# Memory attention with stationary queries, a list scheduler for background work, and no unread matmuls

## The chip, the cores and the metric

One core of one Trainium2 chip. The metric is device time in microseconds (us) of one execution. "Clock" is the share of the TensorE clock that was granted during the execution, as the trace records it.

ScalarE does the exponentials, TensorE (PE) the matmuls, VectorE (DVE) the rest of the arithmetic, GpSimd (POOL) the masks. PE writes to eight PSUM banks of 128 x 512 f32.

## The reference, cut to what matters

Four layers over 2048 tokens of width 512, 32 heads of 16: A, B, A, B. Each is `x + layer(layernorm(x))`. B is full attention. A is attention within four segments of 512 tokens, causal, mixed by a gate with a read-out of a memory that the earlier segments filled.

```python
# A, for each segment s
p = softmax(q_s @ k_s.T * scale + causal_mask);  a_dot = p @ v_s
a_mem = (phi(q_s) @ M) / (phi(q_s) @ z + 1e-6)          # phi(t) = t + 1 if t > 0 else exp(t)
o = g * a_mem + (1 - g) * a_dot
M += phi(k_s).T @ v_s;  z += phi(k_s).sum(over tokens)
# B
o = softmax(q @ k.T * scale) @ v
```

## The kernel before

A Python program places every instruction of every engine beforehand. It keeps a model clock for each engine (`sc.t["pe"]` and so on), a price for each operation, and derives the semaphore waits from buffers and banks. Scores are made transposed, 128 keys by 512 queries a tile. Two or three tiles (of different heads, on different rows of the array) form a group; one exponential on ScalarE empties the group into SBUF. Two sets of banks alternate, so scores can be one group ahead of the exponential. The softmax sum comes from a 17th column of ones in the values. There are 4736 tiles.

```python
def emit_group(self, tiles, mode):      # scores of 2 or 3 tiles, then their exponential
    ...
    sc.add("pe", ... e.matmul(out, lhsT, rhs, start=True, stop=True) ..., cost=(SC0 if first else SC1))
    o = sc.add("act", lambda e: e.activation(dst, src, ACT.Exp, scale=float(SCALE)), ..., cost=0.065 + W / 1200.0)

while pos < len(stream):                # the main loop
    ...                                 # tiles in a fixed order; what they need is forced if it isn't there
    self.emit_group(tiles, m)
    dl = sc.t["act"] - SC0 - 0.1        # the last moment for the next scores, by the model
    self.fill(dl)                       # values (PV), projections and the rest, until then
    while warm and (2 * util + u1) / 3 < UTIL and sc.t["pe"] + MMC < dl:
        if not self.dummy():            # a 512-column matmul that nobody reads, to keep PE's clock up
            break
```

In `fill`, a projection is a thread that places one matmul at a time and holds its bank meanwhile. A group of value matmuls is placed as soon as the model has its exponentials done. Both go in front of the next scores as long as the model still has those in time.

The softmax here doesn't subtract the row's maximum and nothing guards it: scores larger than these inputs give would overflow.

## Time and profile before

| | |
|---|---|
| time | 2681.61 us, median of 2 runs (2669.08 to 2694.13) |
| ScalarE busy | 2256 us of 2696 (84%) |
| exponentials | 1644, of which 1448 with 1536 columns |
| exponentials waiting for scores | 330 us |
| mean clock | 0.75 |

From the page of the old kernel: busy time of each engine; then, in 40 slices of the span, ScalarE's share and the clock, in tenths; then the chain of waits that ended last.

```profile
PE 2296.5 (85%) x12630; PEld 567.9 (21%) x12630; DVE 715.0 (27%) x1572; ACT 2256.1 (84%) x1731; POOL 237.2 (9%) x568
ACT  2666776998999777777898878679999999999998
PEclk9668866999999875668898778579955565555555
PE 46%; ACT 33%; DVE 11%; issue 5%; DMA 3%; POOL 1%; SPq 1%; ACTq 0%; POOLq 0%; DVEq 0%
ACT pT L966 32%; PE ps L959 13%; PE ps L1047 12%; PE ps L1066 12%; PE ps L609 9%; DMA xT<-xn 2%; DVE lnst L641 1%; DVE T L1098 1%; DVE x_tok L863 1%; SPq L350 1%; DVE oT L1155 1%; PE ps L1085 1%; POOL pT L989 1%; DVE T L1088 1%; DVE q L624 1%
```

L959 are score matmuls, L966 exponentials, L1047 value matmuls, L609 projections, L1066 unread matmuls. ScalarE is the engine with the most to do besides PE, and the chain passes through PE more than through ScalarE: something on PE keeps the exponentials waiting.

Groups of ScalarE instructions of the old kernel, by shape (count, busy us, mean ns of one, idle us before them and its cause):

```profile
L966 ACT ACTIVATE pT<-ps 128x1536 bf16<-128x1536 f32 x1448 | 2030.4, 1451 | 289.6 <-PE ps L959 274.8 <-ACT pT L966 2.2 <-issue 1.4
L966 ACT ACTIVATE pT<-ps 128x1024 bf16<-128x1024 f32 x196 | 201.7, 1029 | 59.0 <-PE ps L959 54.7 <-POOL pT L989 2.5 <-issue 0.3
```

Busy time in stretches of 100 us of the old kernel. The columns are PE, weight loads, DVE, ScalarE and POOL with their instruction counts, then the clock:

```profile
500.00:600.00 100.00, 89.91 (x515) 25.22 (x514) 15.72 (x32) 93.57 (x69) 0.00 (x0) 1.00 0.00 1
1000.00:1100.00 100.00, 96.67 (x418) 18.96 (x418) 12.26 (x27) 74.50 (x53) 6.46 (x16) 0.50 0.00 1
2300.00:2400.00 100.00, 88.25 (x432) 18.05 (x431) 5.61 (x11) 99.54 (x73) 0.00 (x0) 0.55 0.00 1
```

In the first the array is warm and full of unread matmuls; in the second it is cold (clock 0.50) and full of them, and ScalarE falls to 75%; in the third it is cold, has no unread matmuls, and ScalarE looks full.

The timeline of the old kernel in the second stretch (start us, length us, engine, line):

```profile
1002.90 1.45 ACT L966 ACTIVATE pT<-ps 128x1536 bf16<-128x1536 f32 x1 [0.17 <-PE ps L959]
...
1003.32 0.61 PE L1066 MATMUL ps<-wA 128*128 128x512 bf16 x1
...
1004.40 1.94 PE L1066 MATMUL ps<-wA 128*128 128x512 bf16 x3
1004.63 1.45 ACT L966 ACTIVATE pT<-ps 128x1536 bf16<-128x1536 f32 x1 [0.28 <-PE ps L959]
...
1006.27 0.61 PE L959 MATMUL ps<-q,kB 32*128 32x512 bf16 x3
...
1007.04 1.45 ACT L966 ACTIVATE pT<-ps 128x1536 bf16<-128x1536 f32 x1 [0.96 <-PE ps L959]
```

Three unread matmuls take 1.94 us on the cold array, the scores come behind them, and the exponential at 1007.04 starts 0.96 us after ScalarE went idle.

### The profile page before, as it was taken

The page shows a single profiled execution, that of the slowest core. Times are in us where ns is not written, and L with a number is a line of the kernel's source. Part 1 is how long each engine was busy: PE and PEld are TensorE (multiplying, and loading weights), DVE is VectorE, ACT ScalarE, POOL GpSimd, SP SyncE. Part 2 cuts the span into 40 slices and gives each one's busy share as a digit, 9 for nine tenths or more (in the row PEclk, how much of TensorE's full clock was granted, in tenths as well). Part 3 has the DMA queues.
Part 4 walks back from the last instruction along what each step waited for, and adds up shares of the span by engine and source line. Part 5 has one row for each costly group of instructions (what it writes and reads, how often), then busy time and mean ns, then how long its engine had stood idle before and what let it go on. Part 6 is the DMA issues. An engine that isn't in the chain of part 4 may idle for free.

```text
span 2695.8 us, 31759 instructions
## 1 busy us (share of the span) xinstructions
PE 2296.5 (85%) x12630; PEld 567.9 (21%) x12630; DVE 715.0 (27%) x1572; ACT 2256.1 (84%) x1731; POOL 237.2 (9%) x568
## 2 busy tenths in 40 slices
PE   4778788888899789998898888889888888888888
PEld 1122221222222221222222222122211111111111
DVE  4676454203111430223412224341000000000000
ACT  2666776998999777777898878679999999999998
POOL 2431221000011000101001011110000000000000
PEclk9668866999999875668898778579955565555555
DMA  4000000000000000000000000000000000000000
GB/s 125 17 17 9 9 1 9 1 1 16 1 1 1 13 12 1 0 1 9 16 1 1 1 9 9 1 9 1 1 9 1 1 8 1 1 1 8 1 0 8
DMA packets 56178, 21.96 MB, mean 8 GB/s; under 512 B 48864, under 2 KB 55520, under 8 KB 56032
## 3 DMA queue, kind: packets, MB, share of 16 engines
q1 hardware_dynamic: 56032, 19.94, 3.2%
q8 instruction: 101, 1.65, 0.3%
q14 instruction: 45, 0.37, 0.0%
HBM read 6.29 MB, written 2.10 MB: 3 GB/s over the span
## 4 chain that ended last, share of the span: by engine, by line
PE 46%; ACT 33%; DVE 11%; issue 5%; DMA 3%; POOL 1%; SPq 1%; ACTq 0%; POOLq 0%; DVEq 0%
ACT pT L966 32%; PE ps L959 13%; PE ps L1047 12%; PE ps L1066 12%; PE ps L609 9%; DMA xT<-xn 2%; DVE lnst L641 1%; DVE T L1098 1%; DVE x_tok L863 1%; SPq L350 1%; DVE oT L1155 1%; PE ps L1085 1%; POOL pT L989 1%; DVE T L1088 1%; DVE q L624 1%
## 5 line engine op out<-in xcount | busy, mean ns | idle before, releaser
L966 ACT ACTIVATE pT<-ps 128x1536 bf16<-128x1536 f32 x1644 | 2212.2, 1401 | 348.6 <-PE ps L959 329.5
L1047 PE MATMUL ps<-pT,vB 128*17 128x512 bf16 x4096 | 767.2, 485 | 129.7 <-ACT pT L966 100.9
L959 PE MATMUL ps<-q,kB 32*128 32x512 bf16 x4096 | 703.0, 490 | 52.1 <-ACT pT L966 50.5
L1066 PE MATMUL ps<-wA 128*128 128x512 bf16 x1076 | 481.3, 447 | 47.7 <-DVE T L1088 16.5
L1098 DVE STREAM_TRANSPOSE T<-ps 128x512 f32<-128x512 f32 x152 | 108.2, 712 | 1469.3 <-PE ps L1047 1439.1
L989 POOL TENSOR_SCALAR_AFFINE_SELECT pT<-pT 128x256 bf16<-128x256 bf16 (+2 forms) x523 | 209.9, 428 | 1083.2 <-ACT pT L966 1081.7
L1047 PEld LDWEIGHTS ps<-pT,vB 128*17 128x17 bf16 x4096 | 160.7, 89 | 671.9 <-issue 322.4
L959 PEld LDWEIGHTS ps<-q,kB 32*128 32x128 bf16 x4096 | 147.3, 95 | 551.0 <-issue 257.5
L1066 PEld LDWEIGHTS ps<-wA 128*128 128x128 bf16 x1076 | 105.2, 98 | 378.5 <-PE ps L1066 212.8
L1047 PE MATMUL ps<-pT,vA 128*17 128x512 bf16 (+3 forms) x1024 | 90.4, 372 | 52.8 <-DVE vB L624 10.9
L959 PE MATMUL ps<-q,kA 32*128 32x512 bf16 (+3 forms) x1024 | 122.7, 362 | 7.9 <-ACT pT L966 5.3
L609 PE MATMUL ps<-xT,wA 128*128 128x512 bf16 x256 | 87.2, 456 | 43.7 <-DMA xT<-xn 32.6
L609 PE MATMUL ps<-xT,wB 128*128 128x512 bf16 x256 | 88.4, 457 | 17.2 <-DMA xT<-xn 15.1
L863 DVE TENSOR_TENSOR x_tok<-x_tok,ps 128x512 bf16<-128x512 bf16 x64 | 44.0, 687 | 101.2 <-PE ps L609 101.2
L609 PE MATMUL ps<-woA,oT 128*128 128x512 bf16 x128 | 50.2, 514 | 17.3 <-DVE oT L1155 16.1
L609 PE MATMUL ps<-woB,oT 128*128 128x512 bf16 x128 | 46.6, 484 | 6.7 <-DVE oT L1155 5.9
L959 PEld LDWEIGHTS ps<-q,kA 32*128 32x128 bf16 x1024 | 29.6, 96 | 92.8 <-issue 47.5
L624 DVE CAST kB<-ps 128x512 bf16<-128x512 f32 x29 | 20.0, 689 | 103.8 <-PE ps L609 103.5
L609 PE MATMUL ps<-wB,xT 128*128 128x128 bf16 (+1 forms) x272 | 45.8, 289 | 2.0 <-PE ps L1047 1.4
L1155 DVE STREAM_TRANSPOSE oT<-on 128x512 bf16<-128x512 bf16 x64 | 45.5, 711 | 2.2
L624 DVE CAST q<-ps 128x512 bf16<-128x512 f32 x49 | 33.7, 688 | 45.2 <-PE ps L609 45.2
L1047 PEld LDWEIGHTS ps<-pT,vA 128*17 128x17 bf16 x1024 | 21.7, 89 | 113.5 <-issue 61.9
(70 smaller groups left out, 750.9 us busy)
## 6 DMA issues: line engine op xcount, KB each, us to landing
x_tok<-in_A_x_dram SPq DMA_DIRECT2D x16, 128.0 KB, 5.5
out_dram<-x_tok SPq DMA_DIRECT2D x4, 512.0 KB, 2.9
wB<-in_B_wqkv_dram SPq DMA_DIRECT2D x1, 1536.0 KB, 9.2
xT<-xn SPq DMA_TRANSPOSE x64, 2.4
wA<-in_A_wq_dram SPq DMA_DIRECT2D x1, 512.0 KB, 4.7
wA<-in_A_wk_dram SPq DMA_DIRECT2D x1, 512.0 KB, 5.6
wA<-in_A_wv_dram SPq DMA_DIRECT2D x1, 512.0 KB, 6.5
woA<-in_A_wo_dram SPq DMA_DIRECT2D x1, 512.0 KB, 6.0
```

What stands on the lines that cost most here:

```text
L350: op = self.sc.add_dma("sp", lambda e: e.dma_start(dst, src, transpose=True), bt, reads=reads, writes=writes, deps=deps, name=name)
L609: return self.sc.add("pe", lambda e: e.matmul(out, lhsT, rhs, start=start, stop=stop), reads=reads, bank_ops=[(bank, "w", alloc)], emit=la ...
L624: return self.sc.add("dve", lambda e: e.tensor_copy(dst, src), writes=writes, bank_ops=[(bank, "r", alloc)], name=name, cost=cost_d)
L641: sc.add("dve", (lambda st, xt: lambda e: e.bn_stats(st, xt))(st, xt), reads=[self.b_x[t]], writes=[self.b_ln[u]], name=f"bst{L}_{t}", cos ...
L863: return [sc.add("dve", lambda e: e.tensor_tensor(xt, xt, src, ALU.add), reads=[self.b_x[t]], writes=[self.b_x[t]], bank_ops=[(bank, "r", ...
L959: sc.add("pe", (lambda out, lhsT, rhs: lambda e: e.matmul(out, lhsT, rhs, start=True, stop=True))(out, lhsT, rhs), reads=reads, bank_ops=[ ...
L966: o = sc.add("act", lambda e: e.activation(dst, src, ACT.Exp, scale=float(SCALE)), writes=[self.b_pT[s0 + i] for i in range(n)], bank_ops= ...
L989: om = sc.add("pool", (lambda ap, pat: lambda e: e.affine_select(ap, ap, pattern=pat, compare_op=ALU.is_ge, fill=0.0, base=0, channel_mult ...
L1047: sc.add("pe", (lambda out, v, rhs, start, stop: lambda e: e.matmul(out, v, rhs, start=start, stop=stop, skip_group_check=True))(out, v, r ...
L1066: o = self.sc.add("pe", lambda e: e.matmul(out, self.wA[:, 0, 0:128], self.wA[:, 0, 0:512], start=True, stop=True), reads=[self.b_wA[0]], ...
L1098: o = sc.add("dve", lambda e: e.transpose(T1.rearrange("p b r -> p (b r)"), src), writes=[bT], bank_ops=[(bank, "r", alloc)], name="T1", c ...
L1155: dv(lambda e: e.transpose(dst, onf), [self.b_on[zo]], [self.b_oT[zs][c]], "oT", 0.55)
```

## The change

Its intent, in four parts:

1. No unread matmuls (1076 of them go).
2. A new placer. It always looks first whether the next scores can go; then come values, if three groups of them are waiting; then projections in whole groups of four matmuls, if by the model the next scores still come in time (the "fit test"); then the other values. Scores are taken when what they need is ready, from either of the two layers in progress, and are not forced. Its prices are corrected: DVE operations, and 0.12 us instead of 0.05 for a semaphore.
3. The memory layers' values with queries stationary: 2560 matmuls with a 128-column block of probabilities as weights and 17 moving columns, in place of 1024 with up to 512 moving columns. The result has tokens on partitions, so the f32 transposes go and the normalisation is shorter; the read-out of the memory is made the same way.
4. PE no longer waits on its own semaphore.

```diff
-UTIL = 0.5
-DVE_AHEAD = 3.0
+DVE_AHEAD = 4.0
@@ dependencies
-            if x is not None and x.eng != eng and x.t_end + 0.05 > t0:
-                t0 = x.t_end + 0.05
+            if x is not None and x.eng != eng and x.t_end + 0.12 > t0:
+                t0 = x.t_end + 0.12
-            if x is None:
+            if x is None or (x.eng == "pe" and eng == "pe"):
                 continue
@@ a projection
-            if i:
-                yield ("t", 0.0, cost)
             mm(bank, alloc, i == n - 1)
@@ memory attention's values (cut)
+            for tl in g["tiles"]:
+                for b in tl["pv"]:
+                    ... e.matmul(self.ps[:, o0:o0 + 17], self.pT[:, slot, p0:p0 + 128], v, start=first, ...)
@@ the new main loop (cut)
+            rs = self.group_ready(g) if g is not None else None
+            rp = self.pv_ready()
+            ...  # bg: the first projection ready; fit: max(rs, t + its cost) + SC0 + 0.12 <= sc.t["act"]
+            if rs is not None and rs <= t + eps and not (credit >= 1.0 and bg is not None):
+                self.emit_group(tiles, m); continue
+            if rp is not None and rp <= t + eps and len(self.pvq) >= MAXPV:
+                self.pv_group(); continue
+            if bg is not None and (credit >= 1.0 or fit):
+                self.advance(bg); continue
+            if rp is not None and rp <= t + eps:
+                self.pv_group(); continue
```

## The prediction

> **What bounds the kernel now.** ScalarE. The page: 2256 of 2696 us busy, 1644 exponentials making 2212 of it; by form, 1448 of 128x1536 at 1451 ns and 196 of 128x1024 at 1029 ns. The reference fixes their 4736 tiles and the change keeps the grouping, so about 2256 us is the floor; 440 us is ScalarE idle, of which 330 us is "exponential waits for the score matmul (PE)". Busy time in 100-us windows places it: 0-500 us (layer 0 and the start of layer 1) 179 us; 500-1900 us (rest of layer 1, layer 2) 230 us; 1900-2696 us only 30 us.
>
> In 2000-2600 us there are no unread matmuls, the granted clock is 0.53-0.59, and ScalarE is 95-99.6% busy: pure attention needs no warm array. In 1000-1100 us the clock is 0.50 as well, 80 unread matmuls are issued, PE is 97% busy and ScalarE 75%. The timeline there shows unread matmul, scores, values in turn, about 540 ns each; the extra 540 ns is what the exponential waits for.
>
> **What the change does.**
> - Removes 1076 unread matmuls (481 us of PE busy). The chain of waits puts 12% (some 320 us) on them, but part would only become another wait.
> - Memory-attention values: 1024 matmuls of up to 512 moving columns (90 us busy) become 2560 pairs of 128-column weight load and 17-column matmul. The timeline has 128-column matmuls with fresh 128-column weights about 57 ns apart warm (ten starting within 0.51 us near 1616 us), about 95 cold. Estimate 130 us warm to 245 cold: PE gets worse by 60 to 150 us.
> - DVE: of the memory layers' normalisation the f32 transposes (712 ns), the second chain and its output transpose go (about 245 us by form), about 130 us comes: 115 us less of 715. DVE is seldom last; it helps before 500 us.
> - 32 more DMA transposes (1.2-2.4 us) off the chain.
> - Projections run in whole groups where the model sees room. The model prices a 512-column matmul at 0.22 us, the warm cost; cold it is 0.43. Four cold ones are 1.75 us against a 1.45-us exponential, partly hidden by double buffering.
>
> **Clock.** The Trainium skill, "TensorE: Matmul & The Clock Gate", Part 1, says the clock falls to half without sustained activity; this trace agrees (0.53-0.59 without filler). So I expect a lower mean clock, about 0.6 instead of 0.75, and a faster kernel all the same.
>
> **Sum.** Floor 2256. Before about 480 us: some 140 us idle (was 179), still PE- and latency-bound. Middle: 95 us (was 230): filler gone, cold projection groups and the weight-load pairs keep the rest. Tail: 25 us (was 30). Total 2516, say 2510 us, 6% faster; range 2420 to 2620. Faster by over 2%: 0.88; within 2%: 0.09; slower: 0.03.
>
> **Right or wrong by.** ScalarE share about 90% and its busy time within 30 us of before; the former 1000-1130 us stretch above 90% ScalarE though cold; PE busy down by 250 us or more; mean clock below 0.7; DVE busy about 600 us; the wait of exponentials for scores falling from 330 to about 170 us; few exponentials of under 1024 columns.
>
> **What would make it wrong.** Cold, the layer-0/1 start being PE-bound: the pairs do not warm the array and the first 500 us grow. Projection groups of four cold matmuls stalling ScalarE by over 1 us each, some 150 times. Or, better than I think: dense projections warm the array by themselves and the middle loses almost nothing (2430 us). Groups broken up by readiness add about 0.2 us of ScalarE time each.

## The result, and the profile after

The new kernel takes 2347.56 us (2347.01 to 2348.11, 2 runs), against 2681.61 of the old one: a ratio of 0.8754, interval 0.8578 to 0.893. The ratios here are the mean time of one kernel's fast runs over that of the other's of the same rounds, so not quite the ratio of the medians. A second measurement with more runs gave 2345.95 us and 0.8732 (0.871 to 0.8753). It is twice the predicted gain, and lies below the predicted range.

The same lines of the page for the new kernel (L878 scores, L883 exponentials, L512 projections, L968 values of B, L956 values of A):

```profile
PE 1797.4 (77%) x13072; PEld 463.7 (20%) x13138; DVE 598.4 (26%) x1370; ACT 2179.2 (93%) x1721; POOL 230.8 (10%) x560
ACT  2878698999999989999999899999999999999997
PEclk8768776558555675566755695575555555555555
ACT 62%; PE 18%; issue 10%; DVE 5%; DMA 3%; SPq 1%; POOL 1%; ACTq 0%; DVEq 0%; POOLq 0%
```

The chain now passes mainly through ScalarE (62%, was 33%), and the clock is lower (0.61, was 0.75). ScalarE's busy time fell by 77 us although it has the same tiles to do. By shape:

```profile
L883 ACT ACTIVATE pT<-ps 128x1536 bf16<-128x1536 f32 x1446 | 1975.1, 1665 | 79.7 <-PE ps L878 72.4 <-issue 5.0 <-POOL pT L906 0.9
L883 ACT ACTIVATE pT<-ps 128x1024 bf16<-128x1024 f32 x198 | 206.4, 1044 | 9.1 <-PE ps L878 8.7
```

1446 records of 1665 ns on average would be 2408 us one after another, but they cover only 1975 us: they overlap. The record of an exponential is longer than what it takes from the next one. The stretches, with the columns of before:

```profile
600.00:700.00 100.00, 74.64 (x665) 19.57 (x662) 10.03 (x28) 100.00 (x76) 18.37 (x48) 0.50 0.00 1
1700.00:1800.00 100.00, 75.02 (x449) 13.38 (x445) 7.00 (x14) 100.00 (x76) 0.00 (x0) 0.50 0.00 1
```

76 ScalarE instructions in 100 us, all exponentials in the second stretch, where the old kernel had 73 at "99.5% busy". (The count takes in one that began before the stretch; 75 and 72 start within it.) The first stretch has memory attention in it as well and is just as full, at clock 0.50. The timelines say why. First the old kernel near its end, then the new one:

```profile
2359.62 8.39 ACT L966 ACTIVATE pT<-ps 128x1536 bf16<-128x1536 f32 x6
...
2360.41 1.30 PE L1047 MATMUL ps<-pT,vB 128*17 128x512 bf16 x4
2361.12 0.09 PEld L1047 LDWEIGHTS ps<-pT,vB 128*17 128x17 bf16 x1 [0.61 <-ACT pT L966]
...
2361.64 0.61 PE L959 MATMUL ps<-q,kB 32*128 32x512 bf16 x3
```

```profile
1948.52 10.98 ACT L883 ACTIVATE pT<-ps 128x1536 bf16<-128x1536 f32 x8
...
1951.50 0.61 PE L878 MATMUL ps<-q,kB 32*128 32x512 bf16 x3 [0.20 <-ACT pT L883]
...
1952.04 0.61 PE L968 MATMUL ps<-pT,vB 128*17 128x512 bf16 x4
...
1952.85 0.61 PE L878 MATMUL ps<-q,kB 32*128 32x512 bf16 x3 [0.20 <-ACT pT L883]
```

In the old kernel three value matmuls start and the fourth has to wait for a running exponential (0.61 us), and the next scores stand behind it. In the new one the scores start the moment the exponential frees their banks, and the values follow; from one group of scores to the next it is 1.35 us. Six exponentials take 8.39 us in the old one, about 1.39 us each if the last record counts as 1.45; eight take 10.98 us in the new one, about 1.34 each if the last record counts as 1.6.

Finally what ScalarE waited for in the old and in the new kernel (us in total, times, longest):

```profile
ACT pT L966 <- PE ps L959: 329.5, 412, 8.8
```

```profile
ACT pT L883 <- PE ps L878: 112.7, 84, 30.7
```

Where the time came from can be read by progress: the time in which each stretch of score tiles had its exponentials done, worked out from the traces. The order of tiles differs a little between kernels.

```
tiles           old    new
0 to 600       499.5  417.5    layer 0 and the start of layer 1 (from the start of the kernel)
600 to 3200   1457.2 1225.5    layer 1, layer 2 mixed in, start of layer 3
3200 to 4736   727.0  690.7    rest of layer 3, no unread matmuls in either
```

### The profile page after: what moved, and what is told of

Read it like the earlier page. It is cut to its first block, busy times and chain, and to the rows that moved or that the text cites. A ratio compares the mean times of both kernels' runs of the same rounds, so it can differ in the third digit from the quotient of the medians.

```text
span 2346.4 us, 31999 instructions
## 1 busy us (share of the span) xinstructions
PE 1797.4 (77%) x13072; PEld 463.7 (20%) x13138; DVE 598.4 (26%) x1370; ACT 2179.2 (93%) x1721; POOL 230.8 (10%) x560
## 4 chain that ended last, share of the span: by engine, by line
ACT 62%; PE 18%; issue 10%; DVE 5%; DMA 3%; SPq 1%; POOL 1%; ACTq 0%; DVEq 0%; POOLq 0%
ACT pT L883 61%; PE ps L512 8%; PE ps L878 6%; PE ps L968 3%; DMA xT<-xn 2%; PE ps L956 1%; DVE lnst L544 1%; POOL pT L906 1%; SPq L354 0%; DVE x_tok L795 0%; DVE ot L733 0%; DMA oT<-ot 0%; DVE xn L562 0%; DVE T L1033 0%; SPq L376 0%
## 5 line engine op out<-in xcount | busy, mean ns | idle before, releaser
L883 ACT ACTIVATE pT<-ps 128x1536 bf16<-128x1536 f32 (+1 forms) x1646 | 2146.1, 1589 | 120.5 <-PE ps L878 112.7
L878 PE MATMUL ps<-q,kB 32*128 32x512 bf16 x4096 | 798.4, 560 | 400.0 <-ACT pT L883 396.9
L968 PE MATMUL ps<-pT,vB 128*17 128x512 bf16 x4096 | 574.1, 554 | 8.7 <-DVE ot L733 4.5
L1033 DVE STREAM_TRANSPOSE T<-ps 128x512 f32<-128x512 f32 x88 | 63.0, 716 | 1141.8 <-PE ps L968 1141.5
L878 PEld LDWEIGHTS ps<-q,kB 32*128 32x128 bf16 x4096 | 146.5, 98 | 1036.8 <-ACT pT L883 992.5
L878 PE MATMUL ps<-q,kA 32*128 32x512 bf16 (+3 forms) x1024 | 136.3, 404 | 58.6 <-ACT pT L883 56.3
L968 PEld LDWEIGHTS ps<-pT,vB 128*17 128x17 bf16 x4096 | 99.1, 90 | 404.9 <-issue 378.5
L512 PE MATMUL ps<-xT,wA 128*128 128x512 bf16 x240 | 73.5, 436 | 37.0 <-DMA xT<-xn 26.2
L956 PE MATMUL ps<-vA,pT 128*128 128x17 bf16 x2560 | 91.7, 175 | 10.4 <-DVE ot L733 2.8
L956 PEld LDWEIGHTS ps<-vA,pT 128*128 128x128 bf16 x2560 | 78.9, 102 | 61.4 <-POOL pT L906 43.9
L512 PE MATMUL ps<-xT,wB 128*128 128x512 bf16 x234 | 71.8, 435 | 12.7 <-DMA xT<-xn 8.1
L878 PEld LDWEIGHTS ps<-q,kA 32*128 32x128 bf16 x1024 | 30.5, 100 | 144.1 <-ACT pT L883 117.1
L544 DVE BATCH_NORM_STATS2 lnst<-x_tok 128x6 f32<-128x512 bf16 x64 | 44.3, 693 | 4.5 <-DMA x_tok<-in_A_x_dram 2.8
L562 DVE TENSOR_SCALAR xn<-x_tok,lnmv,lnr 128x512 bf16<-128x512 bf16 x64 | 25.9, 426 | 74.0 <-DMA xT<-xn 61.5
L512 PE MATMUL ps<-woB,oT 128*128 128x512 bf16 x120 | 39.4, 462 | 4.0 <-issue 1.8
L512 PE MATMUL ps<-wB,xT 128*128 128x128 bf16 (+1 forms) x270 | 42.2, 306 | 0.2 <-issue 0.2
```

What stands on the lines that cost most here:

```text
L512: return self.sc.add("pe", lambda e: e.matmul(out, lhsT, rhs, start=start, stop=stop), reads=reads, bank_ops=[(bank, "w", alloc)], emit=la ...
L544: sc.add("dve", (lambda st, xt: lambda e: e.bn_stats(st, xt))(st, xt), reads=[self.b_x[t]], writes=[self.b_ln[u]], name=f"bst{L}_{t}", cos ...
L562: o = sc.add("dve", (lambda xn, xt, mu, r1: lambda e: e.tensor_scalar(xn, xt, mu, r1, op0=ALU.subtract, op1=ALU.mult))(xn, xt, mu, r1), re ...
L878: sc.add("pe", (lambda out, lhsT, rhs: lambda e: e.matmul(out, lhsT, rhs, start=True, stop=True))(out, lhsT, rhs), reads=reads, bank_ops=[ ...
L956: sc.add("pe", (lambda o0, slot, p0, v, first: lambda e: e.matmul(self.ps[:, o0:o0 + 17], self.pT[:, slot, p0:p0 + 128], v, start=first, s ...
L968: sc.add("pe", (lambda out, v, rhs, start, stop: lambda e: e.matmul(out, v, rhs, start=start, stop=stop, skip_group_check=True))(out, v, r ...
```

## The experiments

Theories, as the expectations name them. F: the unread matmuls alone held the old kernel back. O: the order on PE did, values and projections being put ahead of scores. A: the new memory attention is a main source of the gain. W: PE's waits on its own semaphore. O2, R, G, C: the fit test; readiness; whole groups; corrected prices. Kernels of one call ran on the same chip. All 18 runs gave correct results. The new kernel itself ran as a control in the third call only. Runs of the other calls are compared with that control across chips, by medians; by their ratios to the old kernel of their own call, the differences come out otherwise, by 13 to 15 us in the second and fourth calls. Both are given where it matters, the one by ratios worked out at 2675 us for the old kernel.

### First call: taking the old kernel towards the new one

**No unread matmuls.**

```diff
-UTIL = 0.5
+UTIL = 0.0
```

> The old kernel with its filler threshold set to zero, so no unread matmul; all else old. Theory F (the unread matmuls alone held the kernel back): 2400 us or less, nearly all of the gain. Theory O (the order on PE is the main thing: the old placer puts value matmuls and projections ahead of the next score matmuls): the stretch that was cold with filler gets faster, but projections now meet a cold array, so 2540 to 2640 us; the last 1536 tiles take the same 727 us as before, since no filler was there.

Measured 2544.39 us, ratio 0.9478 (0.9428 to 0.9528), against 2682.27 for the old kernel: 138 us of the 335. Theory F falls. As expected from O, the last 1536 tiles gained nothing (725 us; 727 in the old kernel). The chain of waits had put 12% of the span, some 320 us, on these matmuls; taking them away alone gave 138.

**And no waits of PE on itself.**

```diff
-            if x is None:
+            if x is None or (x.eng == "pe" and eng == "pe"):
```

> As the run without filler, and PE no longer waits on its own semaphore (one line of the change). Theory W (these waits hold back weight loads and scores): over 1% faster than the run without filler. Theory O: within 1% of it, as what they wait for is long done.

Measured 2531.83 us, ratio 0.9435 (0.9388 to 0.9481). The interval overlaps that of the run above; theory W is worth some 0.5%, not told from noise.

**Without unread matmuls, and values behind the next scores.**

```diff
+            self.pv_lim = ends[-2] + 0.01      # end of the exponential before the last
             self.emit_group(tiles, m)
+            ends.append(sc.t["act"])
@@ fill
-            pv_ready = bool(self.pvq) and self.pvq[0]["t"] <= tpe + 0.05
+            pv_ready = bool(self.pvq) and self.pvq[0]["t"] <= min(tpe + 0.05, self.pv_lim)
```

> As the run without filler, and a group of value matmuls is not placed before the exponential after its own has started being modelled, so that the next score matmuls stand ahead of it on PE. Theory O: the last 1536 tiles fall from 727 us towards the 691 us of the new kernel (below 705), exponentials start every 1341 ns there, and the whole is 40 to 120 us faster than the run without filler. Theory F or the memory-attention theory A: no change beyond 1%.

Measured 2476.85 us, ratio 0.9221 (0.9178 to 0.9264): 67 us below the run without unread matmuls. The last 1536 tiles took 698 us, the new kernel's 691 nearly reached. Most of what the end of the kernel gained (28 of 36 us) is this order alone, in a stretch where ScalarE was "99.5% busy". A stretch of that part, first of the run without unread matmuls, then of this one:

```profile
2200.00:2300.00 100.00, 88.72 (x431) 18.45 (x432) 8.35 (x15) 96.39 (x70) 0.00 (x0) 0.55 0.02 6
```

```profile
2200.00:2300.00 100.00, 75.35 (x450) 16.15 (x448) 9.75 (x18) 97.99 (x74) 0.00 (x0) 0.55 0.02 6
```

At the same clock, ScalarE passes 74 instructions instead of 70.

**The new kernel with the old memory attention.** The tiles, the read-out, the normalisation and the two f32 transposes of the old kernel, under the new placer.

```diff
-        if t0["u"]["kind"] == "A":                  # 17 moving columns, queries stationary
-            ...
+        for n in range(max(len(tl["pv"]) for tl in g["tiles"])):   # 512 moving columns, values stationary
+            ...
+        if "nd" in tl and tl["u"]["s"] > 0:
+            self.emit_nd(tl["u"], tl["nd"])
```

> The new kernel with the old memory attention put back (values moving in 512 columns with the values stationary, read-out by feature-major matmul, two f32 transposes and the long normalisation on DVE), under the new list scheduler. Theory O: within 2% of the new kernel, 2330 to 2395 us, with DVE about 115 us busier and PE about as busy. Theory A (query-stationary memory attention and token-major norm are a main source of the gain): 2440 us or more, the loss lying in the first 600 tiles and in layer 2.

Measured 2348.26 us, ratio 0.8746 (0.8706 to 0.8786), the new kernel's time. The busy line of this run:

```profile
PE 1776.9 (76%) x11473; PEld 403.2 (17%) x11554; DVE 714.9 (31%) x1585; ACT 2185.1 (93%) x1734; POOL 232.6 (10%) x561
```

DVE does 117 us more than in the new kernel. PE waits for it longer (51 us in all instead of 37), and so does ScalarE (11 us instead of 7.5), but the time is the same. Theory A falls: under the new placer, the part of the change that stands first in its title is worth nothing in time. Under the old placer it was not tried.

### Second call: taking parts away from the new kernel

**Values ahead of scores.**

```diff
+            if rp is not None and rp <= t + eps:
+                self.pv_group()
+                continue
             if rs is not None and rs <= t + eps and not (credit >= 1.0 and bg is not None):
                 ...                                 # scores
-            if rp is not None and rp <= t + eps and len(self.pvq) >= MAXPV:
-                self.pv_group()
-                continue
```

> The new kernel, but a group of value matmuls that is ready by the model goes ahead of ready score matmuls, as in the old placer. Theory O (scores first): the last 1536 tiles grow from 691 us towards the old 727 us (over 710), the exponentials start later than every 1341 ns, the whole is 40 to 120 us slower, 2390 to 2470. Rival (the order does not matter, only how much work PE has): within 1% of the new kernel.

Measured 2411.68 us, ratio 0.9032 (0.9011 to 0.9053), 66 us above the new kernel (80 by ratios). The last 1536 tiles took 715 us. A stretch of its last part:

```profile
2000.00:2100.00 100.00, 89.81 (x430) 17.48 (x430) 4.90 (x10) 99.66 (x72) 0.00 (x0) 0.52 0.00 1
```

PE looks busier (90% against 75%) and ScalarE full, and 72 instructions go through instead of 75 or 76. Together with the run that moved the values in the old kernel, it shows the order of values and scores from both sides: 67 us on one chip there, 66 to 80 here.

**No fit test.**

```diff
-                        if rs is None or max(rs, t + th.state[2]) + SC0 + 0.12 <= sc.t["act"]:
+                        if True:
```

> The new kernel without its fit test: a projection group is placed whenever its operands are ready by the model, whether or not the next scores still come in time. Theory O2 (the fit test is what saves the rest of the middle): 50 to 130 us slower, the loss in tiles 600 to 3000, the last quarter nearly unchanged. Rival R (readiness of scores, not the fit test): within 1% of the new kernel.

Measured 2337.65 us, ratio 0.8756 (0.8737 to 0.8774). That is 8 us below the new kernel by medians and 6 above it by ratios: the fit test is worth nothing that can be told; theory O2 falls.

**Fixed interleaving of the layers**: the swap to the other layer's unit when one isn't ready is removed (three lines).

> The new kernel, with the units of the two layers in a fixed interleaving: no swap to the other layer's unit when the first isn't ready. Rival R: over 1% slower (2375 us or more), the loss before tile 1000. Theory O2: within 1% of the new kernel.

Measured 2353.81 us, ratio 0.8819 (0.8797 to 0.8842). By medians 0.3% (8 us) above the new kernel, by ratios 1% (23 us); the old kernel was 0.5% faster in this call than in the next, and that is most of the difference. The loss isn't before tile 1000 (599 us there, the new kernel 604) but in the mixed part of layer 2. Readiness in this sense is worth little; without a control in this call, the 1% that theory R asked for is neither shown nor ruled out.

**610 unread matmuls put back**, at most one after each group of scores and only where the model has PE idle.

```diff
+            if self.may_fill and self.filler(min(nxt)):
+                continue
             sc.t["pe"] = min(nxt)
```

> The new kernel with 610 unread matmuls put back, at most one after each group of scores and only into time in which the model has PE idle, in layers 0 to 2 and the first quarter of layer 3. If a warm array is worth its matmuls: faster than the new kernel by over 1%. If the array's clock does not matter once scores stand first: within 1%, at a higher mean clock. If unread matmuls cost because they are real work on a cold array: over 1% slower, ScalarE waiting for scores in the middle.

Measured 2390.43 us, ratio 0.8952 (0.8932 to 0.8972), 44 us slower (59 by ratios). The stretch from 600 to 800 us, first of this run, then of the new kernel:

```profile
600.00:800.00 200.00, 188.88 (x1267) 47.06 (x1264) 31.15 (x74) 190.66 (x140) 26.59 (x66) 0.56 0.03 6
```

```profile
600.00:800.00 200.00, 150.17 (x1198) 37.40 (x1198) 30.53 (x74) 197.30 (x147) 25.76 (x66) 0.55 0.03 6
```

PE has 39 us more to do, the clock hardly moves (0.56 against 0.55), and 7 fewer instructions get through ScalarE. An unread matmul is real work here: 92 of the 99 in this stretch ran at the half clock, at which the next scores start 0.54 us after one (median of the run), over twice its price of 0.22 us in the model. And it hardly warms the array.

### Third call: what of the rest is order

With it ran the new kernel as a control:

> The new kernel once more, as a control on the same chip and rounds as the others: ratio to the old kernel 0.872 to 0.882, from which the others of this call are judged.

Measured 2345.95 us, ratio 0.8732 (0.871 to 0.8753).

**The old placer's deadline rule in the new placer**: scores are held back to the last moment, everything else goes first.

```diff
             rs = self.group_ready(g) if g is not None else None
+            if rs is not None:
+                rs = max(rs, sc.t["act"] - SC0 - 0.2)
```

> The new kernel, but its scores are held back until the last moment at which the model still has them in time for the next exponential, and everything else goes in before them: the old placer's rule inside the new one. Theory O in full (what is left of the gain is that projections, too, stand behind the scores): 2480 to 2540 us, back to about the old kernel without filler, the exponentials of the middle and the last quarter both waiting for scores. Rival (whole groups, readiness and the interleaving matter more than order): under 2430 us.

Measured 2422.41 us, ratio 0.9012 (0.8987 to 0.9037), 76 us slower than the control. It is only 11 us above the run with values alone ahead (across chips; by ratios it is 5 us below it). So the order of projections adds little to that of values, and order in all is worth about 76 us, not 140. Here my expectation was wrong.

**The old kernel without unread matmuls, filled one exponential less far.**

```diff
-            dl = sc.t["act"] - SC0 - 0.1
+            ends.append(sc.t["act"])
+            dl = ends[-2]
```

> The old kernel without filler, with one number of the placer changed: the room after an exponential is filled only until the exponential before it ends, so that values and projections all stand behind the next scores. Theory O in full: 2380 to 2430 us, most of the new kernel's gain, the last quarter at the 691 us of the new kernel. Rival: not better than the run that moved the value matmuls alone (2477 us).

Measured 2484.61 us, ratio 0.9252 (0.922 to 0.9284): no better than moving the values alone. The last 1536 tiles reached 696 us, but the first 600 took 485 (462 with values alone moved): with less room, more of the projections had to be forced when scores needed them.

**An attempt at a faster version: late loads.** The output and second-layer weights, and the tokens of the last two segments, are loaded after the first four transposes instead of before.

```diff
-        for s in range(1, 4):
-            ld_x(s)
-        ...                                # beta, woA, wB, woB
+        ld_x(1)
+        def late_loads(): ...              # x 2 and 3, beta, woA, wB, woB; called at the end of the first layernorm
```

> An attempt at a faster version: the new kernel with the loads of the later weights and of two thirds of the later tokens issued after the first four transposes, which now wait about 9 us behind them. The first exponential should start 6 to 9 us earlier than 32.7 us and the whole be 4 to 9 us faster than the new kernel, the ratio to the old one 0.002 to 0.004 lower. Rival: the start is hidden by later waits and nothing is gained.

Measured 2341.35 us, ratio 0.8716 (0.8699 to 0.8733). The first exponential starts at 23.5 us (control 33.7) and the last ends 7.6 us earlier in the profiled run; the medians differ by 4.6 us, and the intervals overlap. DMA issues of the new kernel, then of this one (a row merges issues that follow one another, so the first row has the first four transposes and four later ones):

```profile
12.61 25.90 SPq L354 DMA_TRANSPOSE xT<-xn  x8
```

```profile
10.26 5.53 SPq L354 DMA_TRANSPOSE xT<-xn  x4
15.84 3.90 SPq L376 DMA_DIRECT2D x_tok<-in_A_x_dram  x8
```

In the new kernel the first two transposes took 9.06 and 6.10 us from issue to landing, in this run 2.50 and 2.48.

### Fourth call: prices and whole groups

What remained between the old kernel without unread matmuls with values moved (2477) and the new one (2346) was 131 us.

**Corrected prices in that old kernel**: DVE, ScalarE and mask work as the trace has it, 0.12 us for a semaphore, DVE allowed 4 us ahead.

> The old kernel without filler and with values behind the scores (2477 us), and its placer given the new one's durations: DVE, ScalarE and mask work as the trace has them (a 0.36-us scale was priced 0.22), 0.12 us for a semaphore instead of 0.05. Theory C (wrong durations let ScalarE and PE queue up behind DVE work that is late): 30 to 90 us faster than 2477, less ScalarE waiting for the memory features (22 us there). Rival G or R: within 1%.

Measured 2446.81 us, ratio 0.9162 (0.9139 to 0.9184): 30 us faster (16 by ratios, as the two ran on different chips). The loss at the start stayed: the first 200 tiles still took 239 us (new kernel 193).

**The old prices in the new kernel.**

> The new kernel with the old placer's durations. Theory C: 30 to 90 us slower than 2346, lost before tile 600 and where layer 2 is mixed in. Rival: within 1%, as PE, not DVE, sets the order and the new placer's rules are robust.

Measured 2361.73 us, ratio 0.8839 (0.8824 to 0.8855): 16 us slower (29 by ratios). Theory C is right in direction from both sides, at 16 to 30 us, below or at the low end of the size expected of it.

**Projections one matmul at a time**, each with its own fit test, the bank held until the last.

```diff
         for i, mm in enumerate(mms):
+            if i:
+                bank.t_free = 1e9
+                yield ("pe1", 0.0, cost)
             mm(bank, alloc, i == n - 1)
```

> The new kernel, its projections placed one matmul at a time, each with its own fit test, a bank held until the last. Theory G (whole groups are better, since a bank is held shorter and its eviction comes earlier): 20 us or more slower than 2346. Rival: within 1%, or faster, as smaller pieces fit the gaps better on a cold array.

Measured 2365.88 us, ratio 0.8855 (0.8837 to 0.8872): 20 us slower (33 by ratios). Whole groups help, at the low end of what theory G expected.

**Late loads, and matmuls priced cold.**

```diff
-MMC = 0.22
-SC0, SC1 = 0.33, 0.02
-PV0 = 0.33
-PB = 0.048
+MMC = 0.43
+SC0, SC1 = 0.54, 0.02
+PV0 = 0.54
+PB = 0.1
... (cut: parts of a score tile at 1200 columns per us instead of 2400)
```

> The version with late loads (ratio 0.8716), its placer pricing matmuls at the cold clock (0.43 us for 512 columns, 0.54 for a group of scores or values, 0.1 for a weight-load pair). If misplaced projections on a cold array still cost ScalarE time: 10 to 40 us faster, ratio 0.857 to 0.868. If the placement is already good enough, or the array is warm just where projections run: within 0.5%; if too cautious prices starve the projections: slower.

Measured 2659.21 us, ratio 0.9952 (0.9935 to 0.9969), nearly the old kernel's time. A stretch of it (columns as above), then what ScalarE waited for (us in total, times, longest):

```profile
1100.00:1200.00 100.00, 57.61 (x525) 22.05 (x527) 42.91 (x109) 38.36 (x34) 21.55 (x54) 0.50 0.06 11
```

```profile
ACT pT L889 <- PE ps L884: 346.1, 91, 33.9
```

91 waits of 3.8 us on average, the longest 33.9, and neither PE nor ScalarE busy. I read it so: with cold prices a group of four is 1.72 us and the scores behind it 0.54, more than an exponential, so the fit test has no room for it; the projections are put off until scores need them, and then the whole path from projection to scores lies open. To see whether it is the test or the prices:

> Late loads, cold prices, no fit test. If it is the fit test that starves the projections at cold prices: back to 2320 to 2360 us. If the cold prices themselves do the harm: above 2500 us.

Measured, without the fit test, 2351.12 us, ratio 0.8799 (0.8785 to 0.8812). So the fit test did the harm, 308 us of it. That most of these prices are nearer to the trace does not help (a projection matmul of 512 columns takes 426 ns at the half clock; but a weight-load pair takes 28 ns, not 100). At warm prices and without the test it is

> Late loads and no fit test, at the warm prices: 2330 to 2342 us, not above the version with late loads (2341 us); the fit test was worth nothing in the new kernel.

Measured 2333.08 us, ratio 0.8734 (0.872 to 0.8747; the old kernel took 2672.98 in this call). It is the lowest time of all, 13 us below the control, but on another chip; by ratio it equals the new kernel. Whether it beats it is not settled. Cold prices are 0.7% worse than warm ones on the same chip.

## Why the prediction was right or wrong

The direction was right, the size was not: 2510 us predicted, 2346 to 2348 measured, below the range of 2420 to 2620. The sum was 2256 + 140 + 95 + 25 = 2516. Measured from the new trace, the same terms are ScalarE busy 2179, and idle 111 before 400 us, 41 from there to 1600 us, and 16 after: 2347. (The stretches are shifted, as the kernel is shorter.) So of the 169 us that the sum missed, 77 are the floor, 54 the middle, 29 the start and 9 the tail.

- **The step that failed first: "2256 us is the floor".** It took the busy time of ScalarE for what its work costs, and put it within 30 us of before; it fell by 77. An exponential that is waited for has a record of 1451 ns; a queued one starts about 1341 ns after the one before. 4736 tiles in threes at 1341 ns are 2117 us, and 49 us of other ScalarE work makes 2166: an estimate of the floor, 90 us below mine. The Trainium skill had it: "ScalarE: Activation LUTs", section "What ACT_TABLE_LOAD costs", says that an activation with immediate scale and bias takes 186 ns + 0.833 ns a column, and "Back-to-back ACTIVATEs overlap by ≈ 93 ns". This agrees: 1466 ns by that formula (an estimate), 1451 measured; an overlap of 110 ns.
- **From the same reading: "1900 to 2696 us only 30 us".** I took 99.5% busy for nothing to gain. The last 1536 tiles fell from 727 to 691 us; the order of values and scores alone brought them from 725 to 698.
- **"Middle: 95 us" was too high** (41). I kept a charge for cold projection groups. It did not come. I read it so: placed behind the scores, a group is hidden by the second set of banks; no run isolates that. It is not the fit test that hides it, as the run without it shows; and the test at cold prices is ruinous.
- **"Some 140 us" at the start was too high** (111). Cause not isolated; part is the 6 us by which the first exponential starts earlier (32.7 us instead of 38.7).
- **"PE gets worse by 60 to 150 us" by the weight-load pairs was wrong.** I took the 57 to 95 ns between 128-column matmuls. These pairs have only 17 moving columns: in the new trace 16 of them take 0.60 us with a last record of 0.18, about 28 ns a pair, though the clock is 0.50. All 2560 are 91.7 us of PE busy time; the 1024 matmuls that they replace were 90.4. The line, from the timeline of the new kernel:

```profile
656.42 0.60 PE L956 MATMUL ps<-vA,pT 128*128 128x17 bf16 x16
```

- **"DVE is seldom last; it helps before 500 us".** DVE fell to 598 us as forecast (about 600). It helped nowhere that can be told: the new kernel with 715 us of DVE takes the same time.
- **Right:** the clock falls (0.61, forecast 0.6) and the kernel is faster all the same; PE busy fell by 499 us (forecast over 250); few exponentials became small (2 of 512 columns); ScalarE's share is 93% (forecast about 90), and it is 100% busy in stretches at clock 0.50 (forecast over 90%). The wait for scores fell further than forecast: 113 us, not 170.
- **The unread matmuls** were the main single cause, at 138 us alone, but I gave them nearly all of the 135 us of the middle and did not see the order at all.

What each part is worth, then: unread matmuls 138 us (taken from the old kernel); values behind scores 67 (from the old), 66 to 80 (from the new); corrected prices 16 to 30; whole groups 20 to 33; the swap between layers 8 to 23; waits on itself some 13, not told from noise; the memory attention, under the new placer, about nothing. That leaves some 80 us between 2447 and 2346 after whole groups that no single run isolated (the swap between layers and the waits on itself may be part of it). They lie in the first 200 tiles (46 us, comparing the old kernel with corrected prices with the new) and in the part with layer 2 mixed in (tiles 2000 to 3000, 45 us). The placer's not forcing scores whose operands are missing is the part of the change that was not tested by itself; that it is the cause is only argued. A rival is open too: in tiles 2000 to 3000 of the old kernel with corrected prices DVE does 196 us of work, against 158 in the new one, and the old memory attention, which is 117 us of DVE work in the whole kernel, was tried only under the new placer.

## What to carry to other kernels

An engine that is 99.5% busy in the trace may still be paced by another: count its instructions per 100 us, or the distance from start to start, before calling its busy time a floor. Where one engine feeds the bottleneck, put what it needs next ahead of everything else on the feeder, and let the rest follow as soon as it can; holding it back until a model's deadline cost 76 us here, and a fit test at other prices starved the work it means to keep away, which cost 308. Work that only keeps a clock up should be tested by leaving it out.

## What the Trainium skill lacked or had wrong

- "Perfetto Trace Analysis", "Identifying the Most-Contended Engine", calls ScalarE's occupancy a fair measure of how close it is to its roofline. Here 99.5% occupancy passed 73 instructions in 100 us, and 100% passed 76 (72 and 75 started within); the records of the new kernel's exponentials, 1665 ns on average, cover 1366 ns each.
- "TensorE: Matmul & The Clock Gate", Part 1, has the clock released after about one busy window of 3.4 us. In the old kernel the clock stayed at 0.50 from 984 to 1120 us, with PE busy 97% by the trace and 80 unread full-array matmuls in 100 of these us (scores start 539 ns after an unread matmul where the trace has the half clock, 322 where it has the full one, in medians); and 610 of them moved the mean clock of the new kernel from 0.61 to 0.64 only. What counts as busy for the gate, with scores on 32 rows and values on 17 columns, no page says.
- The same page, "LDWEIGHTS", gives P / 1.2 ns, 107 ns for 128 columns; "Weight-path perf modes" has a fast load that is about twofold as measured, 53 ns by estimate. Pairs of a bf16 128-column load and a 17-column matmul follow each other faster than either here, and hardly slower at the lower clock: every 27.8 ns at the half clock (mean of 1663) and every 25.9 at the full one (744), of pairs less than 60 ns apart.
